# Blocks of experts started at step 5 and run two or three steps behind their choice, in an attention and mixture-of-experts kernel

## The chip, the cores and the metric

The kernel runs on one core of a Trainium2 chip. The metric is device time of one execution in microseconds (us), as the median over runs. All times are of that one core. The engines are named as the profile names them: PE multiplies matrices (PEld is its loading of the stationary operand), ACT and DVE work on elements, POOL issues the indirect DMAs here, and SP issues the plain ones. Each engine works through its own list of instructions in the order in which the program was laid out, and waits on semaphores for the others.

## What is computed

The reference joins two stages. The first is an attention over channels, for each of 4 batches with N = 5056 rows and C = 256 channels:

```python
qn = q / (norm(q, axis=1) + 1e-06)        # columns normalised over the N rows
kn = k / (norm(k, axis=1) + 1e-06)
a  = softmax(kn.T @ qn / tau)             # 256 x 256 for each batch
x  = v @ a                                # N x 256
```

The 4 × 5056 = 20224 rows of x are the tokens of the second stage, a mixture of 8 experts of which each token takes one:

```python
logits = x @ w_gate + modality_bias[modality_id]
e_idx  = argmax(logits, axis=1)
gate   = softmax(logits)[token, e_idx]
for e in range(8):
    mask = e_idx == e
    out[mask] = gate[mask] * (relu(x[mask] @ w1[e]) @ w2[e])   # w1: 256 x 1024, w2: 1024 x 256
```

All of it is float32.

## The kernel before, in words

**Precision.** PE multiplies values of a shortened type (fp32r). Each float32 operand is split into a high part (a cast on ACT) and a low part (a subtraction on DVE), and each product is made of three matmuls. So a block's weights must pass through ACT and DVE before PE can use them: `w1r`, `w2r` are what a DMA loaded, `w1h`, `w1l`, `w2h`, `w2l` the split parts.

**Steps.** A batch is worked in 10 steps of 512 rows, so there are 40 steps of va work, numbered g = 0 to 39. Three kinds of work are laid side by side in a step:

- *kq* of the next batch (`kq_pieces`): load q and k, split them, multiply (tiles `g`, L277 and L281). It exists in steps 0 to 29. Batch 0's own kq runs ahead of step 0.
- *va* of this step (`va_pieces`): load v, transpose it (`vtp`, L453), multiply by the softmax (`xp`, L469), copy x, find each token's expert and its position in the expert's list (`rp`, L505 to L507), and scatter the 512 rows of x to the table `xs` in DRAM, by four indirect DMAs on POOL (L401).
- *a block* (`block_pieces`): 512 rows of one expert. `load_w` loads its weights in two halves, `load_x` its rows (`xr`, L575), `split_w` splits the weights, `tr_x` transposes the rows (`xtp`, L624), `m1` makes eight groups of the hidden layer (`hp`, L642, six matmuls a group) and `m2` eight groups of the output (`y`, L658, twelve a group). `finish` scales by the gate and scatters to the output. The `y` of the last group runs behind the next block's first `hp`. The input needs 40 blocks.

At the first step of a batch the softmax of that batch is made as well.

**Choosing.** At the end of a step, `pick` (DVE) chooses an expert that has a full block of rows, and writes its place in `xs` and its number to `pki`. SP must read `pki` before it can issue the block's loads. With `START` = 3 the block of slot i is chosen at the end of step 3 + i. `LAG` = 4: it runs four steps later, so that slot 0 opens step 7 and slot 32 runs in step 39. `block_stream` puts the pieces of a block in order, and spreads over its second half the `prep` of the next: its splits and transposes. The next block's `load` (both halves of the weights, then rows) is issued ahead of the step. `once` runs a list of pieces if it has not run yet, and marks it as run.

**Row loads and the table.** A row load depends on the scatters of all the steps up to its choice. Ahead of the tail, `pad_rows` (L150) writes 512 rows of padding (516 KB, from the tile `pad`) behind the last row of each of the 8 experts, so that blocks which are not full read harmless rows. These eight DMAs are on SP's list, with the weight and row loads.

**The tail.** Behind step 39 the blocks that are left, slots 33 to 39, run one after another. `left_over` holds further blocks under a condition that this input does not meet.

**Order.** The pieces of the streams of a step are interleaved in the program text, and a scheduler then moves instructions within each engine's list. Buffers come from rotating pools: three each for `w1r`, `w2r`, `xr`.

Of the kernel before, what the change touches and what calls it, by code (L numbers as in the profile page):

```python
# [34 lines left out]
def kernel(  # L35
# [30 lines left out]
    BADTOK = 1 << 20  # L66
    NB_MIN = -(-T // BLK)
    NB_MAX = (T + E * (BLK - 1)) // BLK
    LAG = 4

    SELF = {
        "q": [{1, 4, 7}, set(), set(), set()],
        "k": [set(range(NS)), set(range(4)), set(), set()],
    }
    START = 3

    def parts(s):
        return P if s < NS - 1 else PL
# [133 lines left out]
    def kq_pieces(b, s):  # L212
# [4 lines left out]
        def load():  # L217
            if s == 0:
                gram[b] = [
                    ps1.tile([P, 2 * C], F32, tag=f"{'y' if b == 0 else 'g'}{m}", name=f"g{m}_{b}")  # L220
                    for m in range(CH)
                ]
                acc[b] = p1.tile([P, 2, 2 * C], F32, tag="acc", name=f"acc_{b}", bufs=2)
                for n in ("k", "q"):
                    if SELF[n][b]:
                        selfp[n, b] = ps2.tile([P, CH, 2 * P], F32, tag="h", name=f"self{n}_{b}")
                        norm[n, b] = p1.tile([P, CH], F32, tag=f"n{n}", name=f"n{n}_{b}")
            for n, src, tag in (("q", q, "w1r"), ("k", k, "w2r")):
                if (b == 0 and s % 5 >= 2) or (b == 1 and 2 <= s < START + 2):
                    st[n] = p3.tile([P, TT, C], F32, tag=tag, name=f"{n}_{b}_{s}")  # L230
                else:
                    st[n] = p2.tile([P, TT, C], F32, tag=n, name=f"{n}_{b}_{s}")
                rows = src[b, t0 : t0 + pp * TT, :].rearrange("(p t) c -> p t c", t=TT)
                if b == 0 and s == 0:
                    st[n + "rows"] = rows
                else:
                    nc.sync.dma_start(st[n][:pp], rows)
            if b == 0 and s == 0:
                for h in range(2):
                    ts = slice(2 * h, 2 * h + 2)  # L240
                    for n in ("q", "k"):
                        nc.sync.dma_start(st[n][:, ts, :], st[n + "rows"][:, ts, :])

        def split(h):
            ts = slice(2 * h, 2 * h + 2)
            more = h == 1 and (b == 0 or (b == 1 and s < START + 1))
            qs = p2.tile([P, 2, 2 * C], F32R, tag="xh" if more else "qs", name=f"qs_{b}_{s}_{h}")
            ks = p2.tile([P, 2, 2 * C], F32R, tag="xl" if more else "ks", name=f"ks_{b}_{s}_{h}")
            st[h] = (qs, ks)
            for n, t in (("q", qs), ("k", ks)):  # L250
                nc.scalar.copy(t[:pp, :, 0:C], st[n][:pp, ts, :])
                nc.vector.tensor_tensor(  # L252
                    t[:pp, :, C : 2 * C], st[n][:pp, ts, :], t[:pp, :, 0:C].bitcast(F32), ALU.subtract
                )
            a = acc[b]
            for n, o in (("q", 0), ("k", C)):
                if s in SELF[n][b]:
                    continue
                first = h == 0 and s == min(set(range(NS)) - SELF[n][b])
                sq = a[:, :, o : o + C]  # L260
                if not first:
                    if b == 0 or (b == 1 and s < START + 1):
# [3 lines left out]
                nc.scalar.activation(sq[:pp], st[n][:pp, ts, :], AF.Square)  # L266
                if not first:
                    nc.vector.tensor_tensor(a[:pp, :, o : o + C], a[:pp, :, o : o + C], sq[:pp], ALU.add)
# [149 lines left out]

    def slots_by(g):

        return max(0, g + 1 - START)

    first_block = LAG + START

    def va_pieces(b, s):
        pp = parts(s)
        g = b * NS + s
        early = g < first_block
        t0 = s * STEP
        st = {}  # L430

        def load():
            vt = p2.tile([P, TT, C], F32, tag="v", name=f"v_{g}")
            if pp < P:
                z0 = pp // 32 * 32
                nc.vector.memset(vt[z0:], 0.0)
            nc.sync.dma_start(
                vt[:pp], v[b, t0 : t0 + pp * TT, :].rearrange("(p t) c -> p t c", t=TT)
            )
            st["v"] = vt  # L440
            st["vh"] = p2.tile([P, CH, STEP], F32R, tag="vh", name=f"vh_{g}")
            st["vl"] = p2.tile([P, CH, STEP], F32R, tag="vl", name=f"vl_{g}")
            more = g % 2 == 1 and g + 2 < first_block
# [125 lines left out]
    def block_pieces(g, slot, pki, tail):  # L569
# [120 lines left out]
        if slot == NB_MIN - 1:  # L690
# [4 lines left out]
        return {"slot": slot, "load": prep, "prep": prep2, "first": lambda: m1(0), "body": body, "last": last}  # L695


    def run(pieces):
# [39 lines left out]
    for g in range(G):  # L738
        b, s = divmod(g, NS)
        streams = []  # L740
        for gg, blk in waiting:
            if gg <= g - LAG + 1:
                once(blk, "load")
        if len(waiting) > 0 and waiting[0][0] <= g - LAG:
            _, blk = waiting.pop(0)
            streams.append(block_stream(blk, waiting[0][1] if waiting and waiting[0][0] <= g - LAG + 1 else None))
        soft = list(softmax_pieces(b)) if s == 0 and b > 0 else []
        streams.append(soft + (va[g + 1][0] if g + 1 < G else []) + va[g][1])
        if b + 1 < B:
            streams.append(list(kq_pieces(b + 1, s)))  # L750
        _interleave(*streams)
        if waiting and waiting[0][0] <= g - LAG + 1:
            once(waiting[0][1], "load")
            once(waiting[0][1], "prep")
        if s == NS // 2 and b + 1 < B:
            setup_bias(b + 1)
        n = slots_by(g)
        while chosen < n:
            waiting.append((g, block_pieces(g, chosen, pick(g, chosen, False), False)))
# [24 lines left out]
    sure = -(-(T - E * (BLK - 1)) // BLK)  # L784
    more = NB_MAX - NB_MIN + slots_by(G - 1) - min(sure, slots_by(G - 1))

    def left_over(slot, n):
        if n <= 0:
# [8 lines left out]
        with tc.If(lv > 0):  # L797
            for i in range(min(n, 4)):
                blk = block_pieces(G - 1, slot + i, pick(G - 1, slot + i, True), True)
                run(blk["load"] + blk["prep"] + [blk["first"]] + blk["body"] + blk["last"])  # L800
            left_over(slot + 4, n - 4)

    left_over(NB_MIN, more)
# [32 lines left out]
```

## Time and profile before

| What | Value |
| --- | --- |
| runs | median 1270.14 us (1269.83 to 1273.26, 3 runs) |
| the profiled execution's own time | 1270.21 us |
| its span in the trace | 1268.1 us |
| PE busy | 1235.1 us, 97% of the span |
| DVE, ACT, POOL busy | 856.4, 753.0, 348.6 us |
| mean granted clock of PE | 0.992 |
| loads of `w1r` and of `xr` | 80 and 40 |

The span goes from the first to the last instruction that was recorded. The busy time of PE is the union of its matmuls; waits of the other engines cost nothing so long as PE has work. A row of the timeline has the start in us, the duration in us, the engine, the line, the operation with its output and inputs, the number of instructions joined in the row, and in brackets how long the engine had been idle before, and on what it waited.

### The profile page before, as it was taken

What the parts mean: (1) busy time and instruction counts of PE and PEld (TensorE: products, weight loads), DVE (VectorE), ACT (ScalarE), POOL (GpSimd) and SP (SyncE); (2) the same over time, 40 slices, a digit from 0 to 9 for tenths busy, and PEclk for the clock granted to TensorE, in tenths of its full rate; (3) what the DMA queues carried; (4) which work ended last, traced back from release to release, by engine and by line L of the source; (5) the groups of instructions that cost most, each with busy time, mean ns of one, the idle gap of its engine ahead of it and who ended that gap; (6) DMA issues with size and microseconds to landing.
All of it is one profiled execution on the core that took longest, in us unless ns stands there. A gap on an engine that the chain in (4) does not pass through costs nothing.

```text
span 1268.1 us, 24269 instructions
## 1 busy us (share of the span) xinstructions
PE 1235.1 (97%) x8368; PEld 1122.6 (89%) x8368; DVE 856.4 (68%) x2330; ACT 753.0 (59%) x1533; POOL 348.6 (27%) x348
## 2 busy tenths in 40 slices
PE   7998999999999999999999999999999999999994
PEld 6897988999999999999999999999999999999994
DVE  7898967867767767777777776565566655755541
ACT  6876756766666666766666665555555554555441
POOL 0036243232222223222232333222223332221121
PEclk9998999999999999999999999999999999999997
DMA  9759854555555555555555544345444444474300
GB/s 314 250 188 296 277 174 156 158 194 167 183 167 165 171 190 169 162 169 167 167 176 182 182 156 141 136 150 168 143 162 140 162 147 134 152 229 168 134 31 15
DMA packets 113124, 215.34 MB, mean 170 GB/s; under 512 B 16224, under 2 KB 61792, under 8 KB 112992
## 3 DMA queue, kind: packets, MB, share of 16 engines
q1 hardware_dynamic: 97632, 172.11, 43.6%
q0 software_dynamic: 15360, 41.60, 8.6%
q8 instruction: 67, 1.10, 0.4%
q14 instruction: 65, 0.53, 0.1%
HBM read 167.33 MB, written 46.60 MB: 169 GB/s over the span
## 4 chain that ended last, share of the span: by engine, by line
PE 80%; issue 3%; DVE 1%; DMA 1%; POOL 1%; ACT 0%; SPq 0%; POOLq 0%; DVEq 0%; ACTq 0%
PE hp L642 32%; PE y L658 32%; PE xp L469 8%; PE g L277 3%; PE vtp L453 2%; PE xtp L624 2%; PE g L281 2%; POOL out_dram L401 1%; DMA k<-in_k_dram 0%; DMA out_dram<-yo,xr 0%; PE ns L323 0%; PE gw L379 0%; DMA modi<-in_moe_modality_id_dram 0%; DVE hl L646 0%; PE atp L369 0%
## 5 line engine op out<-in xcount | busy, mean ns | idle before, releaser
L658 PE MATMUL y<-w2h,hh 128*128 128x256 f32 x1280 | 360.8, 282 | 0.0
L658 PE MATMUL y<-w2l,hh 128*128 128x256 f32 x1280 | 355.6, 278 | 0.0
L658 PE MATMUL y<-w2h,hl 128*128 128x256 f32 x1280 | 355.3, 278 | 0.0
L401 POOL DMA_INDIRECT xs<-x,pi x160 | 175.2, 1095 | 646.2 <-ACT w1h L613 467.5
L646 DVE SCALAR_TENSOR_TENSOR hl<-hp,hh 128x512 fp32r<-128x512 f32 x320 | 219.6, 686 | 132.5 <-ACT hh L645 131.8
L645 ACT ACTIVATE hh<-hp 128x512 fp32r<-128x512 f32 x320 | 191.9, 600 | 182.4 <-PE hp L642 182.3
L642 PE MATMUL hp<-xh,w1h 128*128 128x512 f32 x640 | 259.4, 406 | 0.2 <-ACT xh L629 0.2
L642 PE MATMUL hp<-xl,w1h 128*128 128x512 f32 x640 | 253.4, 396 | 1.2 <-DVE xl L630 1.2
L642 PE MATMUL hp<-xh,w1l 128*128 128x512 f32 x640 | 253.3, 396 | 0.0
L658 PEld LDWEIGHTS y<-w2h,hh 128*128 128x128 f32 x1280 | 240.3, 188 | 12.9 <-ACT hh L645 0.2
L658 PEld LDWEIGHTS y<-w2l,hh 128*128 128x128 f32 x1280 | 241.4, 189 | 11.5
L658 PEld LDWEIGHTS y<-w2h,hl 128*128 128x128 f32 x1280 | 239.5, 187 | 0.1
L401 POOL DMA_INDIRECT out_dram<-yo,xr x160 | 160.6, 1004 | 191.0 <-ACT yo L669 150.4
L614 DVE TENSOR_TENSOR w2l<-w2r,w2h 128x512 fp32r<-128x512 f32 x160 | 110.5, 691 | 70.5 <-ACT w2h L613 70.4
L642 PEld LDWEIGHTS hp<-xh,w1l 128*128 128x128 f32 x640 | 120.6, 189 | 28.7
L613 ACT CAST w2h<-w2r 128x512 fp32r<-128x512 f32 x160 | 100.2, 626 | 74.0 <-PE y L658 67.2
L614 DVE TENSOR_TENSOR w1l<-w1r,w1h 128x512 fp32r<-128x512 f32 x160 | 109.7, 686 | 49.3 <-ACT w1h L613 48.7
L642 PEld LDWEIGHTS hp<-xl,w1h 128*128 128x128 f32 x640 | 120.6, 189 | 16.1 <-DVE xl L630 1.7
L613 ACT CAST w1h<-w1r 128x512 fp32r<-128x512 f32 x160 | 100.9, 630 | 57.1 <-PE hp L642 56.7
L642 PEld LDWEIGHTS hp<-xh,w1h 128*128 128x128 f32 x640 | 120.2, 188 | 14.6 <-ACT xh L629 0.3
L277 PE MATMUL g<-qs,ks 128*128 128x512 f32 (+1 forms) x320 | 122.4, 405 | 6.5 <-DVE qs L252 5.7
L469 PE MATMUL xp<-ah,vh 128*128 128x264 f32 x320 | 96.3, 301 | 5.4 <-DVE pm L552 2.9
(151 smaller groups left out, 1852.0 us busy)
## 6 DMA issues: line engine op xcount, KB each, us to landing
w1r<-in_moe_w_dram SPq DMA_DIRECT2D x80, 512.0 KB, 3.5
w2r<-in_moe_w_dram SPq DMA_DIRECT2D x80, 512.0 KB, 3.5
xr<-xs SPq DMA_DIRECT2D x40, 516.0 KB, 4.8
v<-in_v_dram SPq DMA_DIRECT2D x36, 512.0 KB, 5.5
q<-in_q_dram SPq DMA_DIRECT2D x35, 512.0 KB, 9.2
k<-in_k_dram SPq DMA_DIRECT2D x35, 512.0 KB, 5.7
xs<-pad SPq DMA_DIRECT2D x9, 516.0 KB, 5.5
xs<-x,pi POOLq DMA_INDIRECT x160, 5.1
```

The lines of the kernel that those rows point to most:

```text
L277: nc.tensor.matmul(g, ks[:pp, t, m * P : (m + 1) * P], qs[:pp, t, :], start=first, stop=False, skip_group_check=True,)
L281: nc.tensor.matmul(g[:, 0:C], ks[:pp, t, C + m * P : C + (m + 1) * P], qs[:pp, t, 0:C], start=False, stop=last, skip_group_check=True,)
L401: ins = nc.gpsimd.indirect_dma_start(out=dst, out_offset=bass.IndirectOffsetOnAxis(ap=idx, axis=0), in_=rows, in_offset=None, bounds_check ...
L453: nc.tensor.matmul(tp[:, t * P : (t + 1) * P], st["v"][:, t, h * P : (h + 1) * P], ident, is_transpose=True, start=t == 0, stop=True, skip ...
L469: nc.tensor.matmul(xp[:, 0:DE], a[:, h, t * P : (t + 1) * P], w[:, h, :], start=i == 0, stop=i == len(seq) - 1,)
L613: nc.scalar.copy(hi, src)
L614: nc.vector.tensor_tensor(lo, src, hi.bitcast(F32), ALU.subtract)
L624: nc.tensor.matmul(tp[:, t * P : (t + 1) * P], st["xr"][:, t, h * P : (h + 1) * P], identr, is_transpose=True, start=t == 0, stop=True, sk ...
L642: nc.tensor.matmul(hp, w[:, h, fs], x[:, h, :], start=i == 0, stop=i == len(seq) - 1)
L645: nc.scalar.activation(hh, hp, AF.Relu)
L646: nc.vector.scalar_tensor_tensor(hl, hp, 0.0, hh.bitcast(F32), ALU.max, ALU.subtract)
L658: nc.tensor.matmul(y, a[:, tsl], w[:, j % 2, :], start=(j == 0 and i == 0 and t % 2 == 0), stop=(j == NJ - 1 and i == 2), skip_group_check ...
```

## The change

The first block now opens step 5 instead of step 7. The rule of choice is `slots_by`: at the end of step g there are g − 1 slots chosen up to step 9, and g − 2 from step 10 on. So slot 0 is chosen at the end of step 2, where it was step 3, and slot i runs in step 5 + i: three steps behind its choice up to slot 7, two behind it from slot 8 on. Slot 34 runs in step 39, and five slots (35 to 39) are left for the tail.

The list of loads is split: `load` is the weights, `rows` the rows. In `block_stream` the next block's `load` stands at the head of this block's body, its `rows` a quarter into it, and its `prep` at four, five, six and seven eighths. The three are marked as run in one go, and put into the body whether or not they had been run already. The places ahead of the tail that call `once` for `load` now call it for `rows` too. Some buffers that were lent to the early steps are lent to steps before 5 instead of 7.

```diff
-    LAG = 4
+    FIRST = 5
...
-    START = 3
...
     def slots_by(g):
 
-        return max(0, g + 1 - START)
-
-    first_block = LAG + START
+        return max(0, g + 1 - (2 if g < NS else 3))
...
-        early = g < first_block
+        early = g < FIRST
...
-        prep = [lambda: load_w(0), lambda: load_w(1), load_x]
+        load = [lambda: load_w(0), lambda: load_w(1)]
...
     def block_stream(blk, nxt):
 
         once(blk, "load")
+        once(blk, "rows")
         once(blk, "prep")
         body = list(blk["body"])
         if nxt is not None:
-            once(nxt, "load")
-            done.add((nxt["slot"], "prep"))
-            at = [len(body) * (i + 4) // 8 for i in range(len(nxt["prep"]))]
-            for o, f in reversed(list(zip(at, nxt["prep"]))):
-                body.insert(o, f)
+            done.update((nxt["slot"], what) for what in ("load", "rows", "prep"))
+            ahead = [(2, f) for f in nxt["rows"]] + [(i + 4, f) for i, f in enumerate(nxt["prep"])]
+            for i, f in reversed(ahead):
+                body.insert(len(body) * i // 8, f)
+            body = nxt["load"] + body
...
-        for gg, blk in waiting:
-            if gg <= g - LAG + 1:
-                once(blk, "load")
-        if len(waiting) > 0 and waiting[0][0] <= g - LAG:
-            _, blk = waiting.pop(0)
-            streams.append(block_stream(blk, waiting[0][1] if waiting and waiting[0][0] <= g - LAG + 1 else None))
+        nxt = waiting[0 if g < FIRST else 1] if g >= FIRST - 1 else None
+        if g >= FIRST:
+            streams.append(block_stream(waiting.pop(0), nxt))
...
+        if g == FIRST - 1:
+            streams.append([lambda: once(nxt, "load"), lambda: None, lambda: once(nxt, "rows"), lambda: None])
         _interleave(*streams)
-        if waiting and waiting[0][0] <= g - LAG + 1:
-            once(waiting[0][1], "load")
-            once(waiting[0][1], "prep")
+        if g == FIRST - 1:
+            once(nxt, "prep")
...
-    for _, blk in waiting:
+    for blk in waiting:
         once(blk, "load")
+        once(blk, "rows")
...
             once(blk, "load")
-            waiting.append((G, blk))
+            once(blk, "rows")
+            waiting.append(blk)
             chosen += 1
-        _, blk = waiting.pop(0)
-        run(block_stream(blk, waiting[0][1] if waiting else None))
+        run(block_stream(waiting.pop(0), waiting[0] if waiting else None))
```

In the changed kernel the same lines are numbered one to three lower. The first place is PE's list at the start of the first block. Before, what stands ahead of slot 0's first `hp` ends with the kq of step 6 (`qs_6_1`):

```order
L281 MATMUL g_1_716<-qs_6_1_1736,ks_6_1_1737 128x256
L277 MATMUL g_1_717<-qs_6_1_1736,ks_6_1_1737 128x512
L281 MATMUL g_1_717<-qs_6_1_1736,ks_6_1_1737 128x256
L624 MATMUL xtp_0_1817<-identr,xr_1663 128x128 x4
L624 MATMUL xtp_1_1824<-identr,xr_1663 128x128 x4
L642 MATMUL hp_0_1883<-xh_1815,w1h_0_1807 128x512
L642 MATMUL hp_1_1900<-xh_1815,w1h_0_1807 128x512
L642 MATMUL hp_0_1883<-xl_1816,w1h_0_1807 128x512
```

After the change it ends with the kq of step 5 (`qs_5_1`) and the counting matmuls of step 4:

```order
L280 MATMUL g_1_717<-qs_5_1_1788,ks_5_1_1789 128x256
L502 LDWEIGHTS trim
L502 MATMUL rp_1464<-oh_1460,trim 128x32
L503 LDWEIGHTS onesb
L503 MATMUL rp_1464<-run_1462,onesb 128x32
L504 LDWEIGHTS onesb
L504 MATMUL rp_1464<-run_1462,onesb 128x8
L621 MATMUL xtp_0_1502<-identr,xr_1410 128x128 x4
L621 MATMUL xtp_1_1509<-identr,xr_1410 128x128 x4
L639 MATMUL hp_0_1540<-xh_1500,w1h_0_1492 128x512
```

One step of kq and two of va that stood ahead of the first block now stand behind its start.

The second place is SP's list at the end of the step loop, where the eight pads are. Before, the rows of slot 36 (`xr_16083`) stand behind the eighth pad, after two halves of weights:

```order
L150 DMA xs<-pad 512x1x258
L598 ISA
L598 DMA w2r_0_16067<-in_moe_w_dram 128x4x256
L150 ISA
L150 DMA xs<-pad 512x1x258
L594 ISA
L594 DMA w1r_1_16070<-in_moe_w_dram 128x2x512
L598 ISA
L598 DMA w2r_1_16071<-in_moe_w_dram 128x4x256
L575 ISA
L575 DMA xr_16083<-xs 128x1032
```

After, the rows of slot 36 are loaded twice. The first load (`xr_16585`) stands ahead of the first pad:

```order
L595 DMA w2r_1_16573<-in_moe_w_dram 128x4x256
L570 TENSOR_LOAD pki_16555
L570 ISA x2
L572 ISA
L572 DMA xr_16585<-xs 128x1032
L149 ISA
L149 DMA xs<-pad 512x1x258
```

The second (`xr_16791`) stands behind the eighth pad, here with the seventh at the top:

```order
L149 DMA xs<-pad 512x1x258
L570 TENSOR_LOAD pki_17606
L570 ISA x2
L795 TENSOR_LOAD lefti_18169
L795 ISA x2
L149 ISA
L149 DMA xs<-pad 512x1x258
L572 ISA
L572 DMA xr_16791<-xs 128x1032
L591 ISA
L591 DMA w1r_0_16973<-in_moe_w_dram 128x2x512
```

The third place is PE's list in the tail. Before, the transposes that read `xr_16083` stand in the middle of the block of slot 35 (`y_35`), between its fourth group of `y` (`hh_3`, `hl_3`) and its sixth of `hp`:

```order
L658 MATMUL y_35_16729<-w2h_1_16642,hh_3_16772 128x256
L658 MATMUL y_35_16729<-w2l_1_16643,hh_3_16772 128x256
L658 MATMUL y_35_16729<-w2h_1_16642,hl_3_16773 128x256
L624 MATMUL xtp_0_16829<-identr,xr_16083 128x128 x4
L642 MATMUL hp_5_16836<-xh_16576,w1h_2_16720 128x512
```

After, the transposes read the second copy, `xr_16791`, and stand behind the last `y` of slot 35 (`hl_7`, the eighth group):

```order
L655 MATMUL y_35_16746<-w2h_3_16808,hl_7_16933 128x256
L655 MATMUL y_35_16746<-w2h_3_16808,hh_7_16932 128x256
L655 MATMUL y_35_16746<-w2l_3_16809,hh_7_16932 128x256
L655 MATMUL y_35_16746<-w2h_3_16808,hl_7_16933 128x256
L621 MATMUL xtp_0_16868<-identr,xr_16791 128x128 x4
L621 MATMUL xtp_1_16887<-identr,xr_16791 128x128 x4
L639 MATMUL hp_0_16992<-xh_16866,w1h_0_16835 128x512
L639 MATMUL hp_1_17049<-xh_16866,w1h_0_16835 128x512
```

So no matmul of slot 36 stands ahead of the end of slot 35.

More of the change, by code (lines that the diff above doesn't have):

```diff
@@ L245, in split @@
             ts = slice(2 * h, 2 * h + 2)
-            more = h == 1 and (b == 0 or (b == 1 and s < START + 1))
+            more = h == 1 and (b == 0 or (b == 1 and s < FIRST - 1))
             qs = p2.tile([P, 2, 2 * C], F32R, tag="xh" if more else "qs", name=f"qs_{b}_{s}_{h}")
@@ L442, in load @@
             st["vl"] = p2.tile([P, CH, STEP], F32R, tag="vl", name=f"vl_{g}")
-            more = g % 2 == 1 and g + 2 < first_block
+            more = g % 2 == 1 and g + 2 < FIRST
             st["x"] = p3.tile([P, TT, XW], F32, tag="xr" if more else "x", name=f"x_{g}")
@@ L694, in block_pieces @@
             last += [lambda: finish(2), lambda: finish(3)]
-        return {"slot": slot, "load": prep, "prep": prep2, "first": lambda: m1(0), "body": body, "last": last}
+        return {"slot": slot, "load": load, "rows": [load_x], "prep": prep2, "first": lambda: m1(0), "body": body, "last": last}
     def run(pieces):
@@ L758 @@
         while chosen < n:
-            waiting.append((g, block_pieces(g, chosen, pick(g, chosen, False), False)))
+            waiting.append(block_pieces(g, chosen, pick(g, chosen, False), False))
             chosen += 1
-    for _, blk in waiting:
+    for blk in waiting:
         once(blk, "load")
+        once(blk, "rows")
     endi = p1.tile([1, E], I32, tag="endi", name="endi")
@@ L774, with full_by @@
             once(blk, "load")
-            waiting.append((G, blk))
+            once(blk, "rows")
+            waiting.append(blk)
             chosen += 1
-        _, blk = waiting.pop(0)
-        run(block_stream(blk, waiting[0][1] if waiting else None))
+        run(block_stream(waiting.pop(0), waiting[0] if waiting else None))
     run(open_blk[0]["last"])
-    sure = -(-(T - E * (BLK - 1)) // BLK)
-    more = NB_MAX - NB_MIN + slots_by(G - 1) - min(sure, slots_by(G - 1))
+    def full_by(g):
+        b, s = divmod(g, NS)
+        return max(0, -(-(b * N + min((s + 1) * STEP, N) - E * (BLK - 1)) // BLK))
+    more = NB_MAX - NB_MIN + max(slots_by(g) - full_by(g) for g in range(G))
     def left_over(slot, n):
@@ L799, in left_over @@
                 blk = block_pieces(G - 1, slot + i, pick(G - 1, slot + i, True), True)
-                run(blk["load"] + blk["prep"] + [blk["first"]] + blk["body"] + blk["last"])
+                run(blk["load"] + blk["rows"] + blk["prep"] + [blk["first"]] + blk["body"] + blk["last"])
             left_over(slot + 4, n - 4)
```

4 lines of the change are left out of this document (2 added, 2 removed).

## The prediction

> **What bounds the kernel now.** I read the page's head and busy times first: how full is the fullest engine?
>
> ```profile
> span 1268.1 us, 24269 instructions
> PE 1235.1 (97%) x8368; PEld 1122.6 (89%) x8368; DVE 856.4 (68%) x2330; ACT 753.0 (59%) x1533; POOL 348.6 (27%) x348
> ```
>
> PE is the bound, and 1268.1 − 1235.1 = 33.0 us is all the time in which it does not work. The windows show where that is: columns are the stretch, its length, busy us of PE, PEld, DVE, ACT and POOL, the granted clock, the DMA share and GB/s.
>
> ```profile
> 90.00:120.00 30.00, 25.07 (x154) 21.06 (x154) 24.60 (x120) 19.48 (x45) 21.45 (x21) 0.91 0.87 277
> 600.00:630.00 30.00, 30.00 (x207) 27.35 (x206) 21.33 (x59) 18.59 (x39) 8.29 (x8) 1.00 0.55 177
> 1110.00:1140.00 30.00, 30.00 (x200) 27.22 (x200) 15.30 (x24) 16.28 (x32) 6.04 (x7) 1.00 0.77 219
> ```
>
> The steady steps (600 to 630) and the tail (1110 to 1140) have no hole; the start (90 to 120) has 4.93 us of it. So a change of order can win only at the start, and can lose anywhere. The chain of waits in order of time gives the prices: start, us, piece. Each pair below is one group of hp in two steps running.
>
> ```profile
> 300.22 1.51 PE hp L642 x6
> 330.09 1.50 PE hp L642 x6
> ...
> 951.01 1.51 PE hp L642 x6
> 978.03 1.51 PE hp L642 x6
> ...
> 1125.54 1.47 PE hp L642 x6
> 1148.62 1.47 PE hp L642 x6
> ```
>
> A step with va, a block and kq takes 29.87 us, one without kq 27.02, a block alone 23.08. So the kq of a step is worth 2.85 us of PE and its va 27.02 − 23.08 = 3.94.
>
> **The change part by part.** Base: the profiled execution took 1270.21 us (span 1268.1 and 2.1 around it), beside a median of 1270.14 for the runs. I sum on 1270.2.
>
> *The move.* Two blocks, 2 × 23.08 us of PE, go from the tail into steps 5 and 6. The matmuls are the same and PE was full in both places: 0. Any gain or loss must come out of PE's idle time.
>
> *The start.* Slot 0 now opens step 5. What releases it in before:
>
> ```profile
> 101.07 0.20 ACT L527 COPY x<-tokid 128x4 int32<-128x4 int32 x1 [3.95 <-DMA xs<-x,pi]
> 101.17 0.61 ACT L251 CAST qs<-q 128x512 fp32r<-128x512 f32 x1
> 101.69 0.61 ACT L251 CAST ks<-k 128x512 fp32r<-128x512 f32 x1
> ...
> 113.51 0.96 PE L624 MATMUL xtp<-identr,xr 128*128 128x128 f32 x8
> 114.68 0.73 PE L642 MATMUL hp<-xh,w1h 128*128 128x512 f32 x2 [0.20 <-ACT xh L629]
> ```
>
> ACT stood for 3.95 us until 101.07, when the scatters of step 2 had landed; the changed kernel needs those same scatters. Behind that copy its ACT order has some 15 casts and squares at a pitch of 101.69 − 101.17 = 0.52 us, and two short copies, before xh is there: about 8.5 us, so xh at 109.6 and the first hp at 110.2, only 4.4 us earlier than 114.68. Before that hp, PE's order now has the va of steps 0 to 4 and the kq of 0 to 5, in place of 0 to 6 and 0 to 6. So 2 × 3.94 + 2.85 = 10.7 us of PE's work is put off, and it starts 4.4 us sooner: the idle time at the start grows by +6.3. Against that, the second block (first hp of slots 1, 2 and 3, and the row that held slot 1's step):
>
> ```profile
> 146.50 0.40 PE L642 MATMUL hp<-xh,w1h 128*128 128x512 f32 x1
> 179.20 0.40 PE L642 MATMUL hp<-xh,w1h 128*128 128x512 f32 x1
> 209.05 0.40 PE L642 MATMUL hp<-xh,w1h 128*128 128x512 f32 x1
> 165.79 0.18 DVE L188 TENSOR_SCALAR m1i<-modi 128x40 int32<-128x40 int32 x1 [5.44 <-DMA modi<-in_moe_modality_id_dram]
> ```
>
> That interval is 32.70 us where the next is 29.85: 2.85 lost as DVE stood 5.44 us for modi (step 5, which now holds the first block, where less waits for DVE). I take half back, −1.4. Start: +5, with ends at +1 (xh needs only half of that ACT queue) and +9 (nothing earlier than now plus all of it).
>
> *Two steps of lag.* The first hp of one step and its pick, a load of weights and its cast, and the first hp of another step with its first cast for the next block:
>
> ```profile
> 392.51 0.40 PE L642 MATMUL hp<-xh,w1h 128*128 128x512 f32 x1
> 393.88 0.16 DVE L560 CAST pki<-pk 1x2 int32<-1x2 f32 x1
> 97.56 0.41 SPq L594 DMA_DIRECT2D w1r<-in_moe_w_dram  x1
> 103.06 0.62 ACT L613 CAST w1h<-w1r 128x512 fp32r<-128x512 f32 x1 [0.21 <-DMA w1r<-in_moe_w_dram]
> 602.44 0.48 PE L642 MATMUL hp<-xh,w1h 128*128 128x512 f32 x1
> 611.37 0.68 ACT L613 CAST w1h<-w1r 128x512 fp32r<-128x512 f32 x1
> 615.31 0.63 ACT L266 ACTIVATE sq_k<-k 128x512 f32<-128x512 f32 x1 [3.26 <-DMA k<-in_k_dram]
> ```
>
> The pick is known 1.4 us into the step; a load issued some 1.3 us behind it and landed 103.06 − 97.56 = 5.5 us later is there at about 8.2. The cast is due 611.37 − 602.44 = 8.9 us into its step. It just fits; and where ACT waited 3.26 us at 615.31, PE had no hole (the window 600 to 630). The rows now wait on SP for the scatters of the step before, about 10 us into the step, and queued behind them are q, k, v and the second half of the weights; I estimate landed at 15, and used at 20, where the transposes stand now. I take 0; the ends are 0 and +1 us in each of 27 steps.
>
> *The end.* Here the change does more than its words. `block_stream` now puts the next block's load and rows in the stream without asking whether they are done, and the lines ahead of the tail loop have done them already: slots 36 to 39 are loaded twice, 4 × (2 MB of weights and 516 KB of rows). The block multiplies the second copy, and on SP the second rows of slot 36 stand behind the eighth pad. In before the eight pads are these (first two, third, last; then the rows of slot 36, SP's waits for them, and the page's row for rows):
>
> ```profile
> 1088.04 0.40 PE L642 MATMUL hp<-xh,w1h 128*128 128x512 f32 x1
> 1095.82 0.62 SPq L150 DMA_DIRECT2D xs<-pad  x1
> 1101.24 0.59 SPq L150 DMA_DIRECT2D xs<-pad  x1
> 1105.76 0.56 SPq L150 DMA_DIRECT2D xs<-pad  x1
> ...
> 1132.43 0.56 SPq L150 DMA_DIRECT2D xs<-pad  x1
> 1135.64 0.35 SPq L575 DMA_DIRECT2D xr<-xs  x1
> SPq L150 <- DMA xs<-pad: 18.9, 7, 3.7
> xr<-xs SPq DMA_DIRECT2D x40, 516.0 KB, 4.8
> ```
>
> Each pad waits for the one before: (1132.43 − 1095.82) / 7 = 5.23 us apiece. The first starts 7.78 us after the last step's block does (1095.82 − 1088.04). In before they run beside four blocks that need none of it. Now the rows' path, from the first hp of slot 35, is: 7.78 until the first pad may go, 0.8 for the first rows load, 8 × 5.23 = 41.8 for eight pads, 4.8 for the rows to land: 55.2. What hides it is only slot 35 itself, behind whose last y PE's order puts the transposes of slot 36: eight groups of hp and of y and the y carried over, 17 × 1.40 = 23.8 us (a group of hp takes about as long, 1.47 at the most of the tail's rows above):
>
> ```profile
> 1127.00 1.40 PE y L658 x12
> ```
>
> PE stands for 55.2 − 23.8 = 31.4 us. Then it starts cold, as at the start: from the transposes at 113.51 to the first y there,
>
> ```profile
> 120.66 0.41 PE L658 MATMUL y<-w2h,hh 128*128 128x256 f32 x1
> ```
>
> are 7.15 us, where a running block needs about 3.7 (0.6 of transposes, two groups of hp, a gap): 3.45 lost. End: +35. Its bounds: pads at the shortest spacing, 4.52, give −5.7 and at the longest of these rows, 5.42, +1.5; rows that land in half the time −2.5; the last pad's landing not waited for −5.2. The copies of 37 to 39 (5 MB in 23 us, 217 GB/s, where the start moved 277) I cost at 0, at most +6.
>
> The restart is also what a rule speaks to. This trace has, after an idle time of 2.86 us, a g matmul at 0.77 us that takes 0.40 before the clock drops:
>
> ```profile
> 102.82 0.39 PE L469 MATMUL xp<-ah,vh 128*128 128x264 f32 x1 [2.86 <-DVE pm L552]
> 103.78 0.40 PE L277 MATMUL g<-qs,ks 128*128 128x512 f32 x1
> 104.82 0.77 PE L277 MATMUL g<-qs,ks 128*128 128x512 f32 x1
> ```
>
> The Trainium skill, page "TensorE: Matmul & The Clock Gate", section "Part 1: The HAM clock gate", has PE at half clock after idleness until about 3.4 us of activity have passed. By that page of the Trainium skill the restart costs an estimated 1.7 us and the sum would be 1308; the row's 3.45 holds waits for xl as well, and I keep it.
>
> **Sum**: 1270.2 + 0 + 5 + 0 + 35 = 1310.
>
> **The rivals.**
> R1, *every step waits*. With two steps of lag the weights reach their cast with 0.7 us to spare, and rows with some 5. If that misses, ACT is late for hh, and PE for y: +1 in 27 steps, 1337. Against it: the 3.26 us wait above cost nothing. 0.07.
> R2, *pads are quicker*. In before SP waited for pads only 18.9 us in 7 turns; the rest of each spacing was weight loads that waited for buffers. If a pad costs 18.9 / 7 + 0.6 = 3.3 us, eight take 26.4, rows are there at 39.8 and PE stands 16.0: 1270.2 + 5 + 16.0 + 3.45 = 1295. Against it: the second weights stand between the pads here too. 0.10.
> R3, *not slower*: the pads do not hold SP. If they were issued without waiting, the rows would go at about 15 us after slot 35 starts and be there at 20, ahead of the 23.8; the turning point is a pad of (23.8 − 4.8 − 8.6) / 8 = 1.3 us. Then no end is lost, and if the start's 4.93 us hole also closes where I have it grow, the sum is 1270.2 + 5 − 6.3 − 1.4 = 1267.5, within noise. For it: a pad takes SP only 0.6 us to issue. Against it: the row of seven waits. 0.05.
> That the change does not do what it says: its order has slot 0 in step 5 and five blocks in the tail, so only the rest, loads made twice, is unsaid; no chance of its own.
>
> **How the numbers follow.** Forecast 0.78, R1 0.07, R2 0.10, R3 0.05. The forecast's own bounds are 1299 (start +1, pads 4.52 and half landing) to 1322 (start +9, pads 5.42, copies +6, less what cannot add up). Taking in R2 reaches down to 1293, and leaves out R1, R3 and the edges: under 2 in 10. A measurement can tell 0.3% (3.8 us) from no change. Faster by that: 0.02, the far side of R3. Same: 0.04, the rest of R3 and a sliver of R2. Slower: 0.94.
>
> **What would show it.** Right: on SP in the last 150 us, eight pads after one rows load for slot 36 and before a second, some 50 us after slot 35's first hp; an idle time of PE of about 31 us that ends at rows; 88 loads of w1 and 44 of rows in the page; first hp near 110; steps of 29.9 and 27.0 as before. Wrong: PE full in the tail; steps longer than those by more than 0.3 us; pads closer than 4.5 us; or a first hp before 106, which would make the start a gain.

## The result, and the profile after

The changed kernel takes 1315.01 us (median of 4 runs, 1312.99 to 1315.13) where the kernel before took 1269.99 beside it (1269.44 to 1273.26, 4 runs): a ratio of 1.034, with a 95% interval of 1.0326 to 1.0352. The prediction said 1310 and slower. In two of the three sets of experiments below the kernel before itself took 1321 and 1309 us, so a run's time is compared only with the kernel before of its own set.

The head of the page after, and its rows for loads (count, KB each, us to landing):

```profile
span 1313.4 us, 24297 instructions
PE 1244.7 (95%) x8368; PEld 1123.8 (86%) x8368; DVE 861.0 (66%) x2330; ACT 748.3 (57%) x1533; POOL 347.0 (26%) x348
...
w1r<-in_moe_w_dram SPq DMA_DIRECT2D x88, 512.0 KB, 5.9
...
xr<-xs SPq DMA_DIRECT2D x44, 516.0 KB, 4.8
...
xs<-pad SPq DMA_DIRECT2D x9, 516.0 KB, 4.9
```

PE has the same 8368 matmuls. It idles 68.7 us (1313.4 − 1244.7), where it idled 33.0, and its busy time grew by 9.6: most of that is matmuls at half clock behind the new idle times (the granted clock is 0.50 from 1171.9 to 1205.8). The 88 and 44 loads are the four blocks that are loaded twice. Of the nine pads one goes at 6.1 us, ahead of all steps; the eight of the tail are the others.

The tail in PE's timeline (first hp of slot 35, a wait inside slot 35, and slot 36; the bracket is the idle time and what ended it):

```profile
1146.08 0.40 PE L639 MATMUL hp<-xh,w1h 128*128 128x512 f32 x1
...
1174.51 0.58 PE L655 MATMUL y<-w2h,hh 128*128 128x256 f32 x1 [5.85 <-ACT hh L642]
...
1200.48 1.23 PE L621 MATMUL xtp<-identr,xr 128*128 128x128 f32 x8 [22.99 <-DMA xr<-xs]
1201.88 1.22 PE L639 MATMUL hp<-xh,w1h 128*128 128x512 f32 x2 [0.17 <-ACT xh L626]
1202.89 0.63 PE L639 MATMUL hp<-xl,w1h 128*128 128x512 f32 x1
...
1206.60 0.28 PE L655 MATMUL y<-w2h,hh 128*128 128x256 f32 x1
```

And SP's timeline in the same stretch: slot 36's rows for the first time, the first and the last pad, and the second rows, on which PE waited:

```profile
1156.19 0.34 SPq L572 DMA_DIRECT2D xr<-xs  x1
1156.74 0.63 SPq L149 DMA_DIRECT2D xs<-pad  x1
...
1192.16 0.55 SPq L149 DMA_DIRECT2D xs<-pad  x1
1196.80 0.37 SPq L572 DMA_DIRECT2D xr<-xs  x1
```

The second rows went 1196.80 − 1146.08 = 50.7 us behind the first hp of slot 35. The first 5.85 us of idle time are ACT's: in its order the casts of the second copy of slot 36's weights stand ahead of the last hh of slot 35, and those weights stood between the pads.

```profile
1171.04 1.14 ACT L610 CAST w2h<-w2r 128x512 fp32r<-128x512 f32 x2 [4.80 <-DMA w2r<-in_moe_w_dram]
```

The start, in PE's timeline: the kq ahead of the first block, the transposes, the first hp, and the first hp of slots 1 and 2. Ahead of it rows of ACT, which stood 6.70 us for the scatters of step 2, and then worked without a wait up to the cast that makes xh for the first hp.

```profile
103.42 0.20 ACT L524 COPY x<-tokid 128x4 int32<-128x4 int32 x1 [6.70 <-DMA xs<-x,pi]
...
111.47 0.61 ACT L250 CAST ks<-k 128x512 fp32r<-128x512 f32 x1
111.98 0.57 ACT L626 CAST xh<-xtp 128x512 fp32r<-128x512 f32 x1
```

```profile
106.00 1.19 PE L276 MATMUL g<-qs,ks 128*128 128x512 f32 x2 [5.54 <-DVE pk L555]
110.12 1.23 PE L621 MATMUL xtp<-identr,xr 128*128 128x128 f32 x8 [0.95 <-DMA xr<-xs]
112.61 1.22 PE L639 MATMUL hp<-xh,w1h 128*128 128x512 f32 x2 [1.27 <-ACT xh L626]
...
142.92 0.40 PE L639 MATMUL hp<-xh,w1h 128*128 128x512 f32 x1
...
174.94 0.40 PE L639 MATMUL hp<-xh,w1h 128*128 128x512 f32 x1
```

A step without kq, from the first hp of slot 31 to that of slot 32 (window view):

```profile
1037.86:1065.04 27.18, 27.18 (x190) 24.68 (x188) 17.58 (x50) 14.49 (x30) 7.86 (x9) 1.00 0.48 153
```

PE is full in it, and it is 27.18 us long where it was 27.02. Put together, with the first hp of slot 35 as the cut, since both kernels have done the same work by then:

| us | before | after | difference | forecast |
| --- | --- | --- | --- | --- |
| to the first hp of slot 35 | 1134.19 | 1146.08 | +11.9 | +5 |
| from there to the end of the span | 133.9 | 167.3 | +33.4 | +35 |

The second row is called the tail below. The tail's size says nothing yet of its cause: the copies made twice, the pads in series, or something else of the shorter lag.

### The profile page after: what moved, and what is told of

It is laid out like the page before. It is cut to its first block, busy times and chain, and to the rows that moved or that the text cites. A ratio compares the mean times of both kernels' runs of the same rounds, so it can differ in the third digit from the quotient of the medians.

```text
span 1313.4 us, 24297 instructions
## 1 busy us (share of the span) xinstructions
PE 1244.7 (95%) x8368; PEld 1123.8 (86%) x8368; DVE 861.0 (66%) x2330; ACT 748.3 (57%) x1533; POOL 347.0 (26%) x348
## 4 chain that ended last, share of the span: by engine, by line
PE 88%; DMA 6%; DVE 2%; ACT 1%; issue 1%; SPq 0%; POOL 0%; POOLq 0%; DVEq 0%; ACTq 0%
PE hp L639 33%; PE y L655 33%; PE xp L466 9%; PE g L276 5%; DMA xs<-pad 3%; PE vtp L450 3%; PE g L280 2%; PE xtp L621 2%; DMA xs<-x,pi 1%; PE selfk L287 1%; DMA k<-in_k_dram 1%; PE ns L322 0%; DMA w1r<-in_moe_w_dram 0%; DMA modi<-in_moe_modality_id_dram 0%; DMA xr<-xs 0%
## 5 line engine op out<-in xcount | busy, mean ns | idle before, releaser
L655 PE MATMUL y<-w2h,hh 128*128 128x256 f32 x1280 | 364.8, 285 | 5.8 <-ACT hh L642 5.8
L400 POOL DMA_INDIRECT xs<-x,pi x160 | 170.8, 1068 | 715.2 <-ACT w1h L610 394.8
L639 PE MATMUL hp<-xh,w1h 128*128 128x512 f32 x640 | 263.1, 412 | 1.4 <-ACT xh L626 1.4
L400 POOL DMA_INDIRECT out_dram<-yo,xr x160 | 163.5, 1022 | 167.5 <-ACT yo L666 126.1
L466 PE MATMUL xp<-ah,vh 128*128 128x264 f32 x320 | 93.4, 292 | 3.5 <-DVE vm L487 3.3
```

The source lines that it names most:

```text
L400: ins = nc.gpsimd.indirect_dma_start(out=dst, out_offset=bass.IndirectOffsetOnAxis(ap=idx, axis=0), in_=rows, in_offset=None, bounds_check ...
L466: nc.tensor.matmul(xp[:, 0:DE], a[:, h, t * P : (t + 1) * P], w[:, h, :], start=i == 0, stop=i == len(seq) - 1,)
L639: nc.tensor.matmul(hp, w[:, h, fs], x[:, h, :], start=i == 0, stop=i == len(seq) - 1)
L655: nc.tensor.matmul(y, a[:, tsl], w[:, j % 2, :], start=(j == 0 and i == 0 and t % 2 == 0), stop=(j == NJ - 1 and i == 2), skip_group_check ...
```

## The experiments

Twelve runs in three sets of four. In each, the tail is measured in that run's own profile, from the first hp of slot 35 to the end, and holds no step, only blocks. The kernel before was traced only beside the first runs of the changed kernel, so in all three sets the tails are compared with that trace.

### First set: what is doubled, and the chain of the pads

The kernel before took 1320.81 us in this set (7 runs).

**Single loads** (e1_guard):

```diff
+            rows = nxt["rows"] if (nxt["slot"], "rows") not in done else []
+            load = nxt["load"] if (nxt["slot"], "load") not in done else []
             done.update((nxt["slot"], what) for what in ("load", "rows", "prep"))
-            ahead = [(2, f) for f in nxt["rows"]] + [(i + 4, f) for i, f in enumerate(nxt["prep"])]
+            ahead = [(2, f) for f in rows] + [(i + 4, f) for i, f in enumerate(nxt["prep"])]
...
-            body = nxt["load"] + body
+            body = load + body
```

> Weights and rows of slots 36 to 39 are loaded once: block_stream leaves out what has run already. Theory A (rows of a tail block stand behind eight pads in series): slot 36's rows now go ahead of the pads, so the hole of 23 us behind slot 35 closes; but slot 37's rows are the next behind the eighth pad, some 50 us after slot 35's first hp, and landed at about 54, while PE is through with slots 35 and 36 at about 47. A hole of some 7 us is left, with a slow restart of 2 to 3: about 1292 us. Theory B (the doubled bytes were the cost, pads cost nothing by themselves): no hole at all, only the loss at the start and in the steps (about 12 us by the first hp of slot 35) is left: 1282 us.

**Rows twice, weights once** (e2_rows_twice): the same, but `rows = nxt["rows"]`.

> Only the rows are loaded twice, the weights once (10 MB a tail shrink to 2). Theory A: PE still multiplies the second rows of slot 36, which stay behind the eighth pad: 1312 to 1316 us, as with both doubled, though the wait of ACT for a second copy of weights (5.85 us on PE) goes, since the wait for rows takes its place. Theory B: nearly all of the doubled bytes are gone, so most of the tail's loss goes: 1282 to 1290 us.

**Weights twice, rows once** (e3_weights_twice): the same, but `load = nxt["load"]`.

> Only the weights are loaded twice, the rows once. Theory A: the hole behind slot 35 closes, and what is left is slot 37's rows behind the pads, as with nothing doubled, perhaps with some 6 us more for second weights that stand between the pads: 1290 to 1300 us. Theory B: the bytes are nearly all still there: 1310 to 1316 us.

**Pads free** (e4_pads_free): all loads doubled as in the changed kernel, and

```diff
         pads.append(ins.ins)
+        tc.declare_no_dep(ins.ins, group="pads", reason="each expert's end has rows of its own")
+        tc.add_to_no_dep_group("pads", ins.ins)
```

> The changed kernel with all loads doubled, but the eight pads, which write rows apart, are no longer made to wait for one another. Theory A: eight pads at some 0.85 us of SP each in place of 5.0; the second rows of slot 36 go about 20 us after slot 35's first hp and land at 26 or so, just behind the end of slot 35 at 24: the hole shrinks from 29 us to a few: 1283 to 1290 us. Theory B: the same bytes in the same stretch, so no gain: 1310 to 1316 us.

| | median us | ratio to before (95%) | tail us |
| --- | --- | --- | --- |
| e1, single loads | 1381.25 | 1.0453 (1.0405 to 1.0502) | 153.1 |
| e2, rows twice | 1393.31 | 1.0564 (1.0521 to 1.0608) | 167.6 |
| e3, weights twice | 1382.02 | 1.0487 (1.0451 to 1.0523) | 152.4 |
| e4, pads free, both twice | 1387.70 | 1.0537 (1.0494 to 1.0579) | 160.4 |

All four missed their absolute numbers by 77 us or more, 51 of it in the kernel before as well, since the steps themselves were longer in this set. The tails can be read: rows twice has the changed kernel's tail (167.6 beside 167.3), weights twice has that of single loads (152.4 beside 153.1). So of what is doubled, the rows cost 14.5 us and the weights nothing, as theory A says; the bytes of theory B are in the weights. The wait of 24.49 us in e2 is the same one as above, and 8.33 us at slot 37 is what is left of it in e1:

```profile
1278.40 1.23 PE L621 MATMUL xtp<-identr,xr 128*128 128x128 f32 x8 [24.49 <-DMA xr<-xs]
```

```profile
1289.04 1.23 PE L621 MATMUL xtp<-identr,xr 128*128 128x128 f32 x8 [8.33 <-DMA xr<-xs]
```

But e4 gained 7 us of tail, not 29: letting the pads go without waiting for one another does little for what is loaded behind them. And e1 still has a tail 19 us longer than before. Both say that the pads cost something by themselves.

The steps of this set are a finding of their own. A step without kq took 34 us in e1, and PE waited in each (window view of one step, and one such wait):

```profile
1061.92:1095.97 34.05, 30.21 (x189) 26.94 (x188) 16.63 (x49) 14.54 (x30) 7.88 (x9) 0.90 0.38 125
```

```profile
1039.77 0.58 PE L655 MATMUL y<-w2h,hh 128*128 128x256 f32 x1 [3.88 <-ACT hh L642]
```

That has the form of R1, the rival in which every step waits; it does not show in the changed kernel's profile above, where a step without kq is full. Whether late weights are behind it can't be read here: the pages of the first and third sets list no time to landing for any load.

### Second set: the tail without the double load, and the lag

The kernel before took 1270.96 us here (7 runs), so this set is at the base of the prediction.

**The changed kernel again** (f1_after), as base:

> The changed kernel itself once more, as the base for the runs beside it, since in the four runs before this one the kernel before took 1321 us in place of 1270 and the changed kernel was not among them. If that execution environment comes again: theory A expects 1380 to 1395 (the tail's 33 us and steps that wait for late weights); otherwise 1313 to 1316 us.

**Single loads** (f2_guard), the kernel of e1:

> Weights and rows of slots 36 to 39 once. Beside the changed kernel of the same call: theory A expects the hole of 23 us behind slot 35 gone and one of some 7 us behind slot 36, 20 to 26 us less in all (about 1292 where the kernel before takes 1270). Theory B (doubled bytes): 33 us less.

**Single loads, pads free** (f3_guard_pads_free), the edits of e1 and e4 together:

> Loads once, and the pads, which write rows apart, do not wait for one another. Theory A: both holes of the tail go, the tail is as in the kernel before, and what is left is the loss up to the first hp of slot 35 (11.9 us in the two profiles): 1280 to 1284 where the kernel before takes 1270, so 33 less than the changed kernel. If a third cost sits in the tail, it shows as a hole behind slots 35 to 37.

**First block in step 7, same lag** (f4_first7): f3, and

```diff
-    FIRST = 5
+    FIRST = 7
...
-        return max(0, g + 1 - (2 if g < NS else 3))
+        return max(0, g + 1 - (FIRST - 3 if g < NS else FIRST - 2))
...
-                if (b == 0 and s % 5 >= 2) or (b == 1 and 2 <= s < FIRST):
+                if (b == 0 and s % 5 >= 2) or (b == 1 and 2 <= s < 5):
...
-            more = h == 1 and (b == 0 or (b == 1 and s < FIRST - 1))
+            more = h == 1 and (b == 0 or (b == 1 and s < 4))
```

> As the one with single loads and free pads, but the first block opens step 7 again (choices two steps later, buffers lent as before), with the same lag of two or three steps and the same order within a step. If the start is the loss (8.6 us at the first hp, less some 2 in the next two steps): 1271 to 1275 where the kernel before takes 1270. If the shorter lag is the loss, the steps stay longer than in the kernel before and it takes 1277 or more.

| | median us | ratio to before (95%) | tail us |
| --- | --- | --- | --- |
| f1, as changed | 1317.44 | 1.0366 (1.0347 to 1.0384) | 169.7 |
| f2, single loads | 1299.17 | 1.0211 (1.0192 to 1.0231) | 151.0 |
| f3, single loads, pads free | 1297.60 | 1.0210 (1.0190 to 1.0230) | 149.9 |
| f4, f3 with first block in step 7 | 1293.69 | 1.0175 (1.0153 to 1.0196) | 195.8 from slot 33, where it was 180.1 |

Single loads are worth 18.3 us, a little under what theory A said (20 to 26); the wait left behind slot 36 in f2 is 12.83 us, where 7 was expected. But f3 was to take 1280 to 1284 and took 1298, and f4 1271 to 1275 and took 1294. Theory A is short of a cause: in both the tail is 16 us longer than before (149.9 − 133.9; 195.8 − 180.1), with nothing doubled and no chain of pads. f4 loses another 8.5 us ahead of its tail (first hp of slot 33 at 1096.5, where it was 1088.0), though its first block opens step 7. There ACT stands for scatters again, and PE stands soon after; the first hp comes at 124.8, where the kernel before has it at 114.7:

```profile
116.23 0.20 ACT L526 COPY x<-tokid 128x4 int32<-128x4 int32 x1 [6.79 <-DMA xs<-x,pi]
```

```profile
120.75 0.21 PE L504 MATMUL rp<-oh,trim 128*128 128x32 bf16 x1 [9.06 <-DVE sm L524]
```

So f4 did not take the start's loss away, and does not separate the start from the lag.

The loss in the tail shows in f3 as an idle time of PE of 11.62 us in slot 36. These are the rows for PE and, in order, for ACT and SP:

```profile
1187.94 0.58 PE L657 MATMUL y<-w2h,hh 128*128 128x256 f32 x1 [11.62 <-ACT hh L644]
```

```profile
1186.78 0.62 ACT L612 CAST w1h<-w1r 128x512 fp32r<-128x512 f32 x1 [13.23 <-DMA w1r<-in_moe_w_dram]
```

```profile
1155.23 0.35 SPq L574 DMA_DIRECT2D xr<-xs  x1
1155.78 13.16 SPq L149 DMA_DIRECT2D xs<-pad  x8
1169.79 1.55 SPq L593 DMA_DIRECT2D w1r<-in_moe_w_dram  x1
```

Weights of slot 37, issued at 1169.79, let the cast go at 1186.78: 17.0 us, where a load of w1 took 5.5 in the median of f3. The eight pads were issued in 13.16 us. The last of them landed 19.2 us after its issue, 30.0 us after the first went (1155.8 to 1166.6 + 19.2 = 1185.8). In the changed kernel, from the first pad to the rows behind the last are 40.1 us. These are the windows of the two stretches, the changed kernel's first; both hold the eight pads and four halves of weights (columns as before: the third number from the end is the granted clock, then the DMA share and GB/s):

```profile
1156.74:1196.80 40.06, 14.91 (x90) 13.32 (x89) 8.49 (x13) 8.41 (x16) 3.89 (x4) 0.69 0.62 200
```

```profile
1155.80:1185.80 30.00, 20.35 (x132) 18.08 (x132) 10.35 (x19) 8.41 (x16) 3.89 (x4) 0.89 1.08 225
```

A share of about 1 means that all 16 engines are busy. In series the pads leave them idle for more than a third of the stretch (0.62); together they fill them, and the stretch gets shorter by 10 us only. So theory C: whether the pads go one by one (5.06 us each in the changed kernel) or together (13.4 us each to land, in the median of f3), what is loaded behind them comes some 30 to 40 us after the first of them. A tail has room for that only if enough blocks were chosen ahead of the pads. With the short lag two are (35 and 36); in the kernel before it was four, and three of them (33 to 35) had their rows ahead of the last pad.

### Third set: theory C

The kernel before took 1309.46 us here (8 runs).

**First block in step 6 and in step 7, choices as in the changed kernel** (g1_first6, g2_first7): the kernel of e1 with `FIRST` = 6 or 7, the buffers of q and k kept as in f4, `slots_by` unchanged. One and two steps more lie between choice and run, and three and four blocks are chosen ahead of the pads.

> Single loads, pads in series, the same choices as the changed kernel (slot 0 at the end of step 2), but the first block opens step 6: one step more between choice and run (three to four), six blocks in the tail, three of them chosen before it. Theory C (the pads take some 30 us of the DMA engines, and the tail needs that many blocks whose loads do not stand behind them): three blocks of 23 us cover it, no hole in the tail; rows of slot 0 are long there when PE comes to it. 1268 to 1275 us where the kernel before takes 1271. Rival (the new order inside the steps costs the time): 1285 us or more, with a longer step.

> The same with the first block in step 7, as in the kernel before, choices one step earlier than there, seven blocks in the tail, four of them chosen before it. Theory C: 1269 to 1274 us where the kernel before takes 1271, tail and start as there. Rival (the order inside the steps): 1285 us or more.

**Small pads** (g3_small_pads): f3 with pads of 128 rows, which leaves out three quarters of the padding.

```diff
-            xs[bass.ds(r, BLK), :].rearrange("(p t) c -> p t c", t=BLK // P),
-            pad.unsqueeze(1).to_broadcast([P, BLK // P, XW]),
+            xs[bass.ds(r, P), :].rearrange("(p t) c -> p t c", t=1),
+            pad.unsqueeze(1).to_broadcast([P, 1, XW]),
```

> Single loads and pads that do not wait for one another, first block in step 5, each pad 128 rows in place of 512 (enough for the last blocks of this input, not for all inputs). Theory C: a quarter of the bytes, so the weights of slot 37, which in the run with whole pads landed 17 us after their issue, land in about 6; the hole of 11.6 us goes and its cold restart: 1280 to 1285 us, about 10 above the kernel before, which is the start and the steps. Rival (slot 37 waits for buffers or for its late choice, not for the pads' bytes): 1295 to 1299 us, as with whole pads.

**A buffer at the start** (g4_xbuf): the kernel of e1, and

```diff
-            more = g % 2 == 1 and g + 2 < FIRST
+            more = g % 2 == 1 and g + 2 <= FIRST
```

> Single loads, pads in series, and x of step 3 gets a buffer of the row pool again, as in the kernel before, so that x of step 5 need not wait for the scatters of step 2. If that wait (5 us of ACT and DVE until 103) sets the first hp: 4 to 6 us less than the same kernel without it (1299), first hp at about 107. If the landing of slot 0's rows sets it (transposes wait for them until 110): no change, 1297 to 1301, first hp at 112 or so, and the idle time of PE only moves from ahead of the last kq matmuls to ahead of the transposes.

| | median us | ratio to before (95%) | tail us |
| --- | --- | --- | --- |
| g1, first block in step 6 | 1322.97 | 1.0108 (1.0059 to 1.0156) | 162.6 from slot 34, where it was 157.0 |
| g2, first block in step 7 | 1316.35 | 1.0056 (1.0019 to 1.0093) | 186.1 from slot 33, where it was 180.1 |
| g3, small pads | 1336.55 | 1.0247 (1.0184 to 1.0311) | 138.7 |
| g4, buffer for x | 1355.60 | 1.0361 (1.0329 to 1.0394) | 150.4 |

Again the absolute numbers missed, by some 42 to 55 us, 39 of it in the kernel before as well, and the tails answer. With a quarter of the padding the tail falls from 149.9 to 138.7, 4.8 above the kernel before. The hole in slot 36 is gone: from its first hp to the next are 23.07 us, where f3 had 37.32. What is left is in slot 35, which takes 27.50 us, with this wait in it:

```profile
1204.13 0.38 PE L657 MATMUL y<-w2h,hh 128*128 128x256 f32 x1 [2.28 <-issue]
```

With whole pads in series but one or two blocks more ahead of them (g1, g2) the tail is 5.6 and 6.0 us longer than before, where with two blocks it was 16 to 19. Again only its first block is long (28.52 and 28.49 us), and all behind it but the last take 23.07 to 23.09. So the tails bear theory C out, and neither leaves 16 us to anything else there. The 4 to 5 us in the first block of all tails of this set are not explained; f3 has 1.2 there (24.32). They look like the set's longer steps and not like the pads: g3 has waits of the same kind in two steps ahead of the tail, 2.30 us until 1116.61 and 2.33 until 1146.92.

The times leave more open than the tails. Theory C had g1 at most 4 us above the kernel before, and it is 13.5 above; 5.6 of that are the tail, and the other 8 lie ahead of it, near the 14 us of the rival (the order inside the steps). g2 is 6.9 above, of which the tail makes 6.0. g3 is 27 above where 9 to 14 were forecast, with 4.8 in the tail.

The third set also suggests how a step depends on the lag when the kernel before takes longer itself: most steps without kq are 28.6 to 29.5 us in g1 and g2 (lag three to five), and 30 to 33 in g3 (two). One such step of g2, in which PE idles 1.1 us:

```profile
1042.73:1071.64 28.91, 27.77 (x189) 24.70 (x188) 16.63 (x49) 14.65 (x30) 8.02 (x9) 1.00 0.39 128
```

g4 tests the start. The changed kernel lends no buffer of the row pool to x of step 3 any more, so that x of step 5 waits for the scatters of step 2. With the buffer back, the wait of 5.54 us ahead of the kq is gone, but the transposes wait for the rows instead:

```profile
108.42 1.23 PE L621 MATMUL xtp<-identr,xr 128*128 128x128 f32 x8 [3.88 <-DMA xr<-xs]
109.87 1.22 PE L639 MATMUL hp<-xh,w1h 128*128 128x512 f32 x2 [0.23 <-ACT xh L626]
```

The first hp comes at 109.9, where the other kernels with the first block in step 5 have it at 111.8 to 115.3. By the first hp of slot 2 it is at 170.1, where f1, f2 and f3 have 172.7, 176.2 and 172.7, and g3, of the same set, 171.5. So the buffer is worth some 2 to 5 us at the first hp and 1 to 6 by slot 2. That lies between its two expectations: ACT's wait set the first hp, and once it is gone the rows' landing does.

## Why the prediction was right, and where its reasons were not

**The move: right.** The same matmuls, and all of the loss is idle time and half clock.

**The start: right in its path, short in one term.** Forecast +6.3 at the first hp and −1.4 behind it. Measured: the first hp came at 112.6, 2.1 us earlier with 10.7 us of work put off, so +8.6; and slots 0 and 1 took 62.33 us (174.94 − 112.61) in place of 64.52, so −2.2. Together +6.4 beside +5. The prediction had some 15 casts on ACT behind the scatters of step 2, 8.5 us until xh. The trace has just that: from the copy at 103.42 to xh at 111.98 are 8.56 us without a wait. The term that was mis-sized is when the scatters let ACT go. It was taken over from the kernel before as 101.07 and was 103.42, and with it the first hp came 2.4 us later than the forecast 110.2. The rows for the transposes landed nearly as late: PE could take them at 110.12, so that xh could have begun at 111.35.

**Two steps of lag: 0, measured about +3.** From first hp to first hp, steps without kq are 0.16 us longer and those with it 0.07 (29.92 beside 29.85), with PE full: 10 × 0.16 + 25 × 0.07. PE's order now breaks a group of hp for the counting matmuls, which may be the reason; no run tested it. The range for this term, up to +1 in each of 27 steps, was not needed at the base of the prediction. Where the kernel before took longer itself, R1's longer steps came in part, with their cause not shown: the kernel of e1 lost 60 us there to the kernel before (1381.25 − 1320.81), and the same kernel in f2 lost 28 (1299.17 − 1270.96). The three terms make some 9.8 of the 11.9 us; the rest was not followed.

**The end: right in size, and half right in cause.** Rows were to go at 50.4 us behind slot 35's first hp and went at 50.7; pads at 5.23 apart and were 5.06 ((1192.16 − 1156.74) / 7); rows to land in 4.8 and PE took them 3.7 us after their issue; idle 31.4, measured 5.85 + 22.99 = 28.8, in two pieces where one was foreseen. The step that failed is "here the change does more than its words", which put all of +35 on loads made twice. Undoing them gave back 18.3 us. The other 16 come of the lag alone: with single loads the hole moves from slot 36's rows to slot 37's rows or weights, since only two blocks cover the pads. The prediction itself had noted that before "they run beside four blocks that need none of it" (three, since the rows of slot 36 went behind the last pad there too, at 1135.64), and did not ask how many the change leaves.

**The restart: 3.45 forecast, 2.4 measured.** From the transposes at 1200.48 to the first y at 1206.60 are 6.12 us, where 3.7 are needed. A 128x512 matmul took 0.60 to 0.63 us up to the one at 1205.46 and 0.41 from 1205.88, so the half clock lasted 5.4 us from the first transpose. The Trainium skill ("TensorE: Matmul & The Clock Gate", "Part 1: The HAM clock gate") gives about 3.4 us of activity for it, by which the restart was put at an estimated 1.7; the trace has 2.4, and the measurement decides.

**The rivals.** R2, pads of 3.3 us: not so, 5.06. R3, pads that do not hold SP: not so in the changed kernel, where SP issued one each 5.06 us. f3 made them so, and 16 us of the tail's loss stayed, since what was loaded behind them then waited for the pads' bytes.

What stays open: why the kernel before took 1309 and 1321 us in two sets, what ACT waited for in the long steps, which the trace puts down to nothing that it names, how much of the loss ahead of the tail in g1 and g3 is the order inside the steps, and why the scatters let ACT go later. No kernel here beat the kernel before; g2, nearest to it, was slower by 0.2 to 0.9%.

## What to carry to other kernels

Before shortening the distance between a choice and its use, list all that must pass in that distance at the far end of the loop, not only in its steady part: here eight writes of 516 KB had been hidden by blocks chosen early, and nothing in the steady steps showed it. When code that marks work as done is split, look for paths that do the work and mark it twice. And a wait that is taken away from a chain of transfers buys time only until the engines that carry them are full: here the pads' stretch went from 40 us to 30, and f3 took no time less than f2 that could be told (1297.60 and 1299.17 us).

## What the runs showed of the hardware

Eight writes of 512 rows of 1032 bytes each, one waiting for the other, landed in 4.9 us each (median) and kept the stretch of 40.1 us in which they went at a DMA share of 0.62. Issued without waiting for one another they landed in 13.4 us each (median), 30.0 us from the first issue to the last landing, at a share of 1.08. Both stretches also hold four halves of weights and the stores of four tiles, so that no run shows what the pads take alone. Weights that SP issued behind the eight took 17.0 us, where the median of the same run is 5.5.

A short wait of PE can cost clock as well. In g3 PE stood for 2.28 us until 1204.13, and its granted clock was 0.50 from 1204.5 to 1207.8; in the kernel before it stood for 2.86 us until 102.82, and the clock was 0.50 from 104.2 to 107.5. Not every such wait did it: behind the 2.30 us until 1116.61 in g3 the clock was 1.00.
